# A retention-plus-experts kernel: batch 0 loaded ahead of the held weights, batch 1's attention moved later in tile 0, fp32 loads with casts on the engines

## Chip, cores, metric

One core of a Trainium2 chip; the rounds ran on several chips, each with the kernel before beside it for the ratio. The metric is the device time of the kernel in microseconds (us). Most executions of one kernel agree to about 0.3%.

Engine names: PE is TensorE, PEld its weight loads, DVE is VectorE, ACT is ScalarE, POOL is GpSimd, SP is SyncE (here only an issuer of DMAs). "Eviction" is the copy of a PSUM tile to SBUF through ACT.

## The reference

Retention attention over 8 batches of 8 heads, 576 positions, 64 dims; its output, as 4608 tokens of 512 features, goes through 4 experts (512 to 1024 to 512, ReLU) that are mixed with given probabilities.

```python
def _attn_ref(q, k, v):                      # (8, 8, 576, 64) each
    scores = scale * np.matmul(q, k.transpose(0, 1, 3, 2))
    Dmat = np.where(rel >= 0, gamma[:, None, None] ** rel[None, :, :], 0.0)
    return np.matmul(scores * Dmat[None], v)

def _moe_ref(x, domain_probs, w1, w2):       # (4608, 512), (4608, 4), (4, 512, 1024), (4, 1024, 512)
    p = domain_probs / (domain_probs.sum(-1, keepdims=True) + 1e-09)
    for e in range(E):
        out += p[:, e:e + 1] * (np.maximum(x @ w1[e], 0.0) @ w2[e])
```

## The kernel before

Nine token tiles of 512 go through the experts. While tile nt runs, the attention of batch nt+1 is woven in, one "unit" (a transpose group, a score group, a state step, an output group) after every second step of the tile. A tile has 48 steps: for each expert eight evictions of the first product (`ph` to `hT`) and four second products (`po`). Weights are cast to bf16 by the DMA.

```python
    load_first()                 # batch 0: k, v, q, two heads at a time, fp32, 24 DMAs on SP's queue
    ...
    for e in range(E):
        load_w(e)                # two cast DMAs of 512 K elements each, on POOL's queue, at once
        if e == 0:
            load_first_rem()
    ...
    nc.sync.dma_start(out=probs, ...)          # behind batch 0 on SP's queue
    # ... cut ...
    def load(b):                 # b >= 1
        for h in range(H):
            nc.sync.dma_start(out=t["k"][:, :, h, :], in_=main_in(k, b, h))       # fp32
        for n, src in (("q", q), ("v", v)):
            for h in range(H):
                nc.gpsimd.dma_start(out=m[:, :, h, :], in_=main_in(src, b, h))    # cast in flight
    # ... cut ...
    att = attention(0)
    next(att)
    next(att)                    # batch 0 up to its last output
    load(1)
    for nt in range(n_nt):
        if nt == 0:
            for _ in att:        # rest of batch 0
                pass
        nxt = attention(nt + 1) if nt + 1 < B else None
        if nxt is not None and nt + 2 < B:
            load(nt + 2)
        n = 0
        for _ in moe(nt):
            n += 1
            if nxt is not None and n >= 3 and n % 2 == 1:
                next(nxt, None)  # batch 1's first units come in expert 0 of tile 0
```

Of the kernel before, what the change touches and what calls it, by code (L numbers as in the profile page):

```python
# [2 lines left out]

# [6 lines left out]
FP32 = mybir.dt.float32  # L10
BF16 = mybir.dt.bfloat16
Copy = mybir.ActivationFunctionType.Copy
Relu = mybir.ActivationFunctionType.Relu
Exp = mybir.ActivationFunctionType.Exp
MULT = mybir.AluOpType.mult
ADD = mybir.AluOpType.add
# [4 lines left out]
def kernel(  # L21
# [10 lines left out]
    nc = tc.nc  # L32
    B, H, S, D = q.shape
    N, E = moe_domain_probs.shape
    _, Dm, F = moe_w1.shape
# [3 lines left out]
    NC_ = S // C  # L39
    R = S - NC_ * C  # L40
    SM = NC_ * C
    NP = H // 2
# [6 lines left out]

    const = ctx.enter_context(tc.tile_pool(name="const", bufs=1))  # L50
    wpool = ctx.enter_context(tc.tile_pool(name="wpool", bufs=1))
    raw = ctx.enter_context(tc.tile_pool(name="raw", bufs=3))
    rawr = ctx.enter_context(tc.tile_pool(name="rawr", bufs=2))
    cast2 = ctx.enter_context(tc.tile_pool(name="cast2", bufs=2))
    att1 = ctx.enter_context(tc.tile_pool(name="att1", bufs=1))
    att2 = ctx.enter_context(tc.tile_pool(name="att2", bufs=2))
    hpool = ctx.enter_context(tc.tile_pool(name="hpool", bufs=2))
    apool = ctx.enter_context(tc.tile_pool(name="apool", bufs=5))
    ps_mm = ctx.enter_context(tc.tile_pool(name="ps_mm", bufs=3, space=PSUM))
    ps_at = ctx.enter_context(tc.tile_pool(name="ps_at", bufs=4, space=PSUM))  # L60
    ps_kv = ctx.enter_context(tc.tile_pool(name="ps_kv", bufs=1, space=PSUM))
# [2 lines left out]
    def main_in(src, b, h):  # L64
        return src[b, h, 0:SM, :].rearrange("(c p) d -> p c d", p=C)

    def rem_in(src, b):
        return src[b, :, SM:S, :].rearrange("h p d -> p h d")

    state = {}  # L70

    def load_first():
        t = {}
        for n, src in (("k", k), ("v", v), ("q", q)):
            t[n] = raw.tile([128, NC_, H, D], FP32, tag="raw", name=f"raw_{n}")
        for p in range(NP):
            for n, src in (("k", k), ("v", v), ("q", q)):
                for h in (2 * p, 2 * p + 1):
                    nc.sync.dma_start(out=t[n][:, :, h, :], in_=main_in(src, 0, h))  # L79
        t["kr"] = rawr.tile([R, H, D], FP32, tag="rawr", name="rawr_k")  # L80
        nc.sync.dma_start(out=t["kr"], in_=rem_in(k, 0))
        state[0] = t

    def load_first_rem():
        for n, src in (("q", q), ("v", v)):
            r = cast2.tile([R, H, D], BF16, tag=f"{n}r", name=f"{n}r")
            nc.gpsimd.dma_start(out=r, in_=rem_in(src, 0))
            state[0][n + "rm"] = r

    def load(b):  # L90
        t = {}
        t["k"] = raw.tile([128, NC_, H, D], FP32, tag="raw", name="raw_k")
        t["kr"] = rawr.tile([R, H, D], FP32, tag="rawr", name="rawr_k")
        for h in range(H):
            nc.sync.dma_start(out=t["k"][:, :, h, :], in_=main_in(k, b, h))
        nc.sync.dma_start(out=t["kr"], in_=rem_in(k, b))
        for n, src in (("q", q), ("v", v)):
            m = cast2.tile([128, NC_, H, D], BF16, tag=f"{n}m", name=f"{n}m")
            r = cast2.tile([R, H, D], BF16, tag=f"{n}r", name=f"{n}r")
            for h in range(H):  # L100
                nc.gpsimd.dma_start(out=m[:, :, h, :], in_=main_in(src, b, h))  # L101
            nc.gpsimd.dma_start(out=r, in_=rem_in(src, b))
            t[n + "m"], t[n + "rm"] = m, r
        state[b] = t

    load_first()


    w1_sb, w2_sb = [], []

    def load_w(e):
        wt1 = wpool.tile([128, NDC, F], BF16, tag=f"w1_{e}", name="wt1")
        nc.gpsimd.dma_start(out=wt1, in_=moe_w1[e].rearrange("(dc p) f -> p dc f", p=128))
        w1_sb.append(wt1)
        wt2 = wpool.tile([128, NFC, Dm], BF16, tag=f"w2_{e}", name="wt2")
        nc.gpsimd.dma_start(out=wt2, in_=moe_w2[e].rearrange("(fc p) d -> p fc d", p=128))
        w2_sb.append(wt2)


    ident = const.tile([128, 128], BF16)  # L120
# [9 lines left out]
    gk = const.tile([128, NC_ + 1, H], FP32)  # L130
# [18 lines left out]
    for n in range(NC_):  # L149
        nc.vector.memset(sbd[n], 0.0)  # L150

    for e in range(E):
        load_w(e)
        if e == 0:
            load_first_rem()


    NTT = N // 128
    probs = const.tile([128, NTT, E], FP32)
    nc.sync.dma_start(out=probs, in_=moe_domain_probs.rearrange("(t p) e -> p t e", p=128))  # L160
    psm = const.tile([128, NTT], FP32)
    nc.vector.tensor_reduce(psm, probs, axis=mybir.AxisListType.X, op=ADD)
    nc.vector.tensor_scalar_add(psm, psm, 1e-9)
    nc.vector.reciprocal(psm, psm)
    nc.vector.tensor_tensor(probs, probs, psm[:, :].unsqueeze(2).to_broadcast([128, NTT, E]), op=MULT)

    xT = const.tile([128, NDC, N], BF16)

# [1 line left out]
    def attention(b):  # L170
        t = state[b]
        first = b == 0
        km = att1.tile([128, NC_, H, D], BF16, tag="km")
        kr = att1.tile([R, H, D], BF16, tag="kr")
        if first:
            qm = cast2.tile([128, NC_, H, D], BF16, tag="qm", name="qm")
            qr, vr = t["qrm"], t["vrm"]
            vm = cast2.tile([128, NC_, H, D], BF16, tag="vm", name="vm")
        else:
            qm, qr, vm, vr = t["qm"], t["qrm"], t["vm"], t["vrm"]  # L180

        def cast_k(h0, h1):
            n = h1 - h0
            for c in range(NC_):
                nc.vector.tensor_tensor(  # L185
                    km[:, c, h0:h1, :], t["k"][:, c, h0:h1, :],
                    gk[:, c, h0:h1].unsqueeze(2).to_broadcast([128, n, D]), op=MULT)

        def cast_first(p):
            h0, h1 = 2 * p, 2 * p + 2  # L190
            cast_k(h0, h1)
            nc.scalar.activation(qm[:, :, h0:h1, :], t["q"][:, :, h0:h1, :], Copy)  # L192
            nc.gpsimd.tensor_copy(vm[:, :, h0:h1, :], t["v"][:, :, h0:h1, :])

        def cast_rem():
            nc.vector.tensor_tensor(
                kr, t["kr"], gk[:R, NC_, :].unsqueeze(2).to_broadcast([R, H, D]), op=MULT)

        qkT = att1.tile([128, 2, NP, S], BF16, tag="qkT")
        kvp = {}  # L200
# [87 lines left out]
        allp = list(range(NP))  # L288
        if first:
            def start(p):  # L290
                cast_first(p)
                U_T(p)
                U_kv(0, [p])

            def mid(p):
                U_S(p)
                for n in range(1, NC_):
                    U_kv(n, [p])
            start(0)
            mid(0)  # L300
            start(1)
            U_O(0)
            mid(1)
            start(2)
            U_O(1)
            yield
            mid(2)
            start(3)
            U_O(2)
            mid(3)  # L310
            U_O(3)
            yield
            cast_rem()
            U_Trem()
            yield
            U_Srem()
            yield
            U_Orem()
            yield
        else:  # L320
            cast_k(0, H)
            cast_rem()
            yield
            for u in (lambda: U_T(0), lambda: U_kv(0, allp), lambda: U_T(1), lambda: U_kv(1, allp),
                      lambda: U_S(0), lambda: U_kv(2, allp), lambda: U_T(2), lambda: U_S(1),
                      lambda: U_O(0), lambda: U_T(3), lambda: U_kv(3, allp), lambda: U_S(2),
                      lambda: U_O(1), U_Trem, lambda: U_S(3), lambda: U_O(2), U_Srem,
                      lambda: U_O(3), U_Orem):
                u()
                yield  # L330


    def moe(nt):
        n0 = nt * NT
        acc = [apool.tile([128, Dm], FP32, tag="acc", name="acc") for _ in range(NSUB)]
        for e in range(E):
            hT = hpool.tile([128, NFC, NT], BF16, tag="hT")
            for fc in range(NFC):
                ph = ps_mm.tile([128, NT], FP32, tag="mm", name="ph")
                for dc in range(NDC):  # L340
                    nc.tensor.matmul(ph, lhsT=w1_sb[e][:, dc, fc * 128:(fc + 1) * 128],  # L341
                                     rhs=xT[:, dc, n0:n0 + NT], start=(dc == 0), stop=(dc == NDC - 1))
                nc.scalar.activation(hT[:, fc, :], ph, Relu)  # L343
                yield
            for ns in range(NSUB):
                po = ps_mm.tile([128, Dm], FP32, tag="mm", name="po")
# [11 lines left out]

    att = attention(0)
    next(att)  # L360
    next(att)
    load(1)
    for nt in range(n_nt):
        units = []
        if nt == 0:
            for _ in att:
                pass
        nxt = attention(nt + 1) if nt + 1 < B else None
        if nxt is not None and nt + 2 < B:
            load(nt + 2)  # L370
        n = 0
        for _ in moe(nt):
            n += 1
            if nxt is not None and n >= 3 and n % 2 == 1:
                next(nxt, None)
        if nxt is not None:
            for _ in nxt:
                pass


# [28 lines left out]
```

## Time and profile before

| | before |
|---|---|
| median time | 641.65 us (16 runs, 639.82 to 642.91) |
| span of the profiled run | 640.1 us |
| PE busy | 572.1 us |
| PE without work | 68.0 us |
| first eviction of tile 0 | 82.38 us |
| period of a tile with attention (first eviction of tile 2 to that of tile 3) | 63.41 us |

PE is the busy engine, so its idle time is the account that most of a gain must come from. The view of busy time by stretch divides it (columns: stretch, length, then busy time of PE, PEld, DVE, ACT, POOL with instruction counts, granted clock, DMA share, GB/s):

```profile
0.00:64.00 64.00, 3.70 (x32) 2.37 (x32) 8.45 (x42) 7.29 (x12) 13.76 (x27) 1.00 1.11 185
64.00:82.38 18.38, 14.58 (x123) 7.79 (x122) 12.27 (x23) 6.55 (x30) 15.25 (x21) 0.98 1.78 168
82.38:145.24 62.86, 62.86 (x408) 29.86 (x408) 24.78 (x39) 24.31 (x44) 23.14 (x32) 0.98 0.97 110
145.24:640.10 494.86, 490.96 (x2961) 231.18 (x2958) 159.21 (x242) 190.25 (x336) 53.21 (x72) 1.00 0.23 33
```

Length minus PE busy is PE's idle time: 60.3 us before 64 us, 3.8 us up to the first eviction, nothing in tile 0, and 3.9 us after it (the tail of the last tile). So nearly all of the 68.0 us lies before the experts begin.

### The profile page before, as it was taken

Reading aid. Unit: us, or ns where it says so; the run is one execution under the profiler, and the core shown is the slowest. Engines: PE = TensorE matmul, PEld = TensorE weight load, DVE = VectorE, ACT = ScalarE, POOL = GpSimd, SP = SyncE. Lnnn points to the kernel's source line nnn. Section 1 sums busy time; section 2 is a strip of 40 time slices with the busy share of each in tenths; the row PEclk is TensorE's granted clock in tenths of the full one; section 3 lists DMA queues with packets and bytes.
Section 4 is the critical chain, followed back from the end, with each engine's and each line's share of the span. In section 5 each row is a group of like instructions: output and inputs, shape, how many; then the busy total and the mean of one; then the engine's idle time right before and its main releaser. Section 6 shows DMA issues by size and latency. Waiting matters only on the chain.

```text
span 640.1 us, 8432 instructions
## 1 busy us (share of the span) xinstructions
PE 572.1 (89%) x3520; PEld 271.2 (42%) x3520; DVE 204.7 (32%) x345; ACT 228.4 (36%) x422; POOL 105.4 (16%) x150
## 2 busy tenths in 40 slices
PE   0110889999999999999999999999999999999997
PEld 0000444444444444444444444454444444444443
DVE  1200633631463146314631463146313420121121
ACT  0300444325332533253325333533353235333332
POOL 5101860440034003401240124000000000000000
PEclk9999989999999999999999999999999999999999
DMA  9999996960096009600570047000100010001001
GB/s 165 193 201 179 166 178 98 111 67 37 1 112 70 34 1 112 72 32 5 42 86 18 6 32 87 18 1 1 52 14 1 1 66 1 2 1 67 0 1 66
DMA packets 130165, 38.36 MB, mean 60 GB/s; under 512 B 119376, under 2 KB 123472, under 8 KB 130128
## 3 DMA queue, kind: packets, MB, share of 16 engines
q0 software_dynamic: 73856, 16.79, 28.2%
q1 hardware_dynamic: 56272, 21.05, 14.8%
q8 instruction: 27, 0.44, 0.3%
q14 instruction: 10, 0.08, 0.0%
HBM read 45.16 MB, written 9.44 MB: 85 GB/s over the span
## 4 chain that ended last, share of the span: by engine, by line
PE 87%; SPq 9%; DMA 2%; POOL 2%; issue 0%; DVE 0%; POOLq 0%
PE ph L341 39%; PE po L348 39%; SPq L79 9%; PE pt L220 2%; PE o L267 2%; PE s L242 1%; DMA vm<-in_v_dram 1%; PE o L271 1%; PE kvp L207 1%; POOL qm L101 1%; DMA raw_v<-in_v_dram 1%; POOL vm L101 1%; PE ptr L229 0%; PE orem L280 0%; PE orem L284 0%; PE sr L255 0%
## 5 line engine op out<-in xcount | busy, mean ns | idle before, releaser
L343 ACT ACTIVATE hT<-ph 128x512 bf16<-128x512 f32 x288 | 171.9, 597 | 299.5 <-PE ph L341 298.2
L341 PE MATMUL ph<-xT,wt 128*128 128x512 bf16 x1152 | 272.9, 381 | 1.4 <-DVE xT L274 1.4
L348 PE MATMUL po<-wt,hT 128*128 128x512 bf16 x1152 | 261.4, 379 | 0.0
L348 PEld LDWEIGHTS <-hT 128*128 128x128 bf16 x1152 | 110.7, 98 | 126.7
L341 PEld LDWEIGHTS <-wt 128*128 128x128 bf16 x1152 | 107.4, 98 | 118.1 <-issue 2.1
L354 DVE SCALAR_TENSOR_TENSOR acc<-po,probs,acc 128x512 f32<-128x512 f32 x108 | 81.1, 751 | 197.8 <-PE po L348 179.6
L101 POOL DMA_DIRECT2D qm<-in_q_dram x56 | 41.7, 771 | 158.1 <-PE pt L220 155.1
L246 DVE TENSOR_TENSOR sT<-s,tri 128x512 bf16<-128x512 f32 x64 | 41.1, 683 | 53.5 <-PE s L242 53.5
L101 POOL DMA_DIRECT2D vm<-in_v_dram x56 | 41.7, 772 | 60.9 <-PE o L271 58.2
L223 DVE COPY qkT<-pt 128x1024 bf16<-128x1024 bf16 x32 | 22.0, 688 | 88.4 <-PE pt L220 88.4
L220 PE MATMUL pt<-ident,qm 128*128 128x128 bf16 x128 | 13.6, 232 | 32.3 <-ACT qm L192 32.3
L207 PE MATMUL kvp<-vm,km 128*128 128x128 bf16 x128 | 15.5, 226 | 27.9 <-ACT sbd L213 25.8
L352 ACT ACTIVATE acc<-po,probs 128x512 f32<-128x512 f32 x36 | 24.7, 687 | 36.8 <-PE po L348 36.8
L185 DVE TENSOR_TENSOR km<-raw_k,gk 128x512 bf16<-128x512 f32 (+1 forms) x44 | 21.4, 542 | 40.5 <-DMA raw_k<-in_k_dram 23.0
L213 ACT ACTIVATE sbd<-kvp 64x256 bf16<-64x256 f32 (+1 forms) x88 | 27.8, 316 | 8.7 <-PE kvp L207 8.1
L274 DVE TENSOR_TENSOR xT<-o,gq 128x512 bf16<-128x512 f32 x32 | 22.0, 686 | 21.5 <-PE o L271 19.5
L220 PEld LDWEIGHTS <-qm 128*128 128x128 bf16 x128 | 10.3, 103 | 39.5 <-ACT qm L192 32.6
L267 PEld LDWEIGHTS <-vm 128*64 128x64 bf16 x256 | 8.8, 111 | 40.0 <-issue 39.9
L192 ACT ACTIVATE qm<-raw_q 128x512 bf16<-128x512 f32 x4 | 2.5, 629 | 39.4 <-DMA raw_q<-in_q_dram 39.4
L242 PE MATMUL s<-qkT 64*128 64x128 bf16 x256 | 13.8, 226 | 2.4 <-DVE qkT L223 2.4
L267 PE MATMUL o<-sT,vm 128*64 128x128 bf16 x256 | 15.0, 231 | 0.0
L207 PEld LDWEIGHTS <-km 128*128 128x128 bf16 x128 | 10.5, 100 | 10.4 <-issue 2.2
(48 smaller groups left out, 117.5 us busy)
## 6 DMA issues: line engine op xcount, KB each, us to landing
out_dram<-acc SPq DMA_DIRECT2D x36, 256.0 KB, 2.0
raw_k<-in_k_dram SPq DMA_DIRECT2D x64, 128.0 KB, 4.6
wt<-in_moe_w_dram POOLq DMA_DIRECT2D x8, 1024.0 KB, 31.1
qm<-in_q_dram POOLq DMA_DIRECT2D x56, 64.0 KB, 3.1
vm<-in_v_dram POOLq DMA_DIRECT2D x56, 64.0 KB, 3.0
raw_v<-in_v_dram SPq DMA_DIRECT2D x8, 128.0 KB, 10.5
raw_q<-in_q_dram SPq DMA_DIRECT2D x8, 128.0 KB, 14.5
rawr_k<-in_k_dram SPq DMA_DIRECT2D x8, 128.0 KB, 3.6
```

The costliest lines, as they stand in the source:

```text
L79: nc.sync.dma_start(out=t[n][:, :, h, :], in_=main_in(src, 0, h))
L101: nc.gpsimd.dma_start(out=m[:, :, h, :], in_=main_in(src, b, h))
L207: nc.tensor.matmul(kvp[g][:, p, :], lhsT=km[:, n, 2 * p:2 * p + 2, :].rearrange("p h d -> p (h d)"), rhs=vm[:, n, 2 * p:2 * p + 2, :].rear ...
L213: nc.scalar.activation(sbd[n][j:j + 64, a:z, j:j + 64], kvp[g][j:j + 64, a:z, j:j + 64], Copy)
L220: nc.tensor.transpose(pt[:, i, c * C:(c + 1) * C], src[:, c, 2 * p:2 * p + 2, :].rearrange("p h d -> p (h d)"), ident)
L246: nc.vector.tensor_tensor(st[:, j], s[j], tri[:, :].unsqueeze(1).to_broadcast([128, NC_, C]), op=MULT)
L267: nc.tensor.matmul(o[64 * j:64 * j + 64, c * C:(c + 1) * C], lhsT=vm[:, c, 2 * p + j, :], rhs=sT[p][:, j, c, :], start=(c == 0), stop=Fals ...
L341: nc.tensor.matmul(ph, lhsT=w1_sb[e][:, dc, fc * 128:(fc + 1) * 128], rhs=xT[:, dc, n0:n0 + NT], start=(dc == 0), stop=(dc == NDC - 1))
L343: nc.scalar.activation(hT[:, fc, :], ph, Relu)
L348: nc.tensor.matmul(po, lhsT=hT[:, fc, ns * 128:(ns + 1) * 128], rhs=w2_sb[e][:, fc, :], start=(fc == 0), stop=(fc == NFC - 1))
L352: nc.scalar.activation(acc[ns], po, Copy, scale=pe)
L354: nc.vector.scalar_tensor_tensor(acc[ns], po, pe, acc[ns], op0=MULT, op1=ADD)
```

## The change

Its intent: give the DMA engines to batch 0 alone at the start, let the weights follow when they are about to be needed, keep all of q, k, v off POOL's queue, and move batch 1's attention to where its data will have arrived. The diff, cut to its core:

```diff
+    nc.sync.dma_start(out=probs, ...)          # the probabilities go first
+    load(0)
...
-    def load_first(): ...   def load_first_rem(): ...   # q, v of b >= 1 by cast DMAs on POOL's queue
+    def load(b):                               # every batch: 24 fp32 DMAs on SP's queue, one buffer each
+    def after(ins, dep): ...                   # an extra semaphore wait of ins on dep
...
+        def cast_pair(p):                      # one cast of a pair on DVE (k), ACT (q) and POOL (v)
+            ck = nc.vector.tensor_tensor(km..., MULT)
+            cq = nc.scalar.activation(qm[:, :, h0:h1, :], t["q"][:, :, h0:h1, :], Copy)
+            gate[b, p] = nc.gpsimd.tensor_copy(vm[:, :, h0:h1, :], t["v"][:, :, h0:h1, :])
+            if b == 1:
+                for i in (ck, cq, gate[b, p]):
+                    after(i, evict[2 + p // 2, 7 if p < 2 else 3])
...
     att = attention(0)
     next(att)
+    w = [load_w(0)]
+    for i in w[0]:
+        after(i, gate[0, 2])                   # weights only after the v cast of batch 0's pair 2
     next(att)
+    w += [load_w(e) for e in range(1, E)]      # (held in the same way)
+    mixing_weights()
+    load_rem(0)
+    for i in load(1)[:1]:
+        after(i, w[0][1])                      # batch 1 after expert 0's second matrix has landed
+    load_rem(1)
     for nt in range(n_nt):
...
+            if nt == 0:
+                if n in (11, 13, 15, 17):
+                    next(att, None)            # the rest of batch 0, inside expert 0 and 1
+                if n == 33 or n == 42:
+                    next(nxt)                  # casts of batch 1, in expert 2 and 3
+                elif n == 44:
+                    next(nxt); load(2); load_rem(2)
+                elif n > 44:
+                    next(nxt, None); next(nxt, None)   # two units per step; the other 11 after the tile
+            else:
+                if n == 12 and nt + 2 < B:
+                    load(nt + 2); load_rem(nt + 2)
+                if n >= 3 and n % 2 == 1:
+                    next(nxt, None)
```

The accumulator pool also goes from 5 to 7 buffers, and the k cast of a pair is one instruction instead of four.

## The prediction

> **What bounds the kernel now.** I read the page from its forty slices, then asked for the first microseconds (what SyncE's queue issues, who waits), then for the period of the steady part.
>
> The slices come first, because the average PE share (89%) hides two different stages:
>
> ```profile
> span 640.1 us, 8432 instructions
> PE 572.1 (89%) x3520; PEld 271.2 (42%) x3520; DVE 204.7 (32%) x345; ACT 228.4 (36%) x422; POOL 105.4 (16%) x150
> PE   0110889999999999999999999999999999999997
> ACT  0300444325332533253325333533353235333332
> DMA  9999996960096009600570047000100010001001
> ```
>
> One slice is 16 us. In the first four (0 to 64 us) PE does almost nothing while the DMA engines are full; from about 86 us on PE has no gap until the end. So there is a start bounded by DMA and then a long stretch bounded by TensorE. The busy time by stretch shows how tight the second is:
>
> ```profile
> 145.24:208.65 63.41, 63.41 (x410) 30.20 (x408) 23.91 (x37) 24.42 (x44) 13.30 (x18) 1.00 0.44 55
> 462.29:525.70 63.41, 63.41 (x409) 30.20 (x408) 20.91 (x32) 24.43 (x44) 0.00 (x0) 1.00 0.05 17
> 525.70:580.96 55.26, 55.26 (x257) 25.05 (x256) 9.01 (x12) 21.86 (x36) 0.00 (x0) 1.00 0.05 20
> ```
>
> The columns are the stretch, its length, then busy time of PE, weight loads, DVE, ACT, POOL, granted clock, DMA share and GB/s. One token tile that also carries a batch of attention takes 63.41 us, all of it PE; a tile without attention takes 55.26; the difference, 8.15 us, is PE work of one batch. Tile 1 starts at 145.24. From there to the end are six tiles of 63.41, two of 55.26 and 3.9 us of tail: 494.9 us, and 145.24 + 494.9 = 640.1. These 494.9 us only change if a tile's period does. The whole question is when tile 1 starts.
>
> The stretch before that is held up by loads. The waits:
>
> ```profile
> ACT qm L192 <- DMA raw_q<-in_q_dram: 39.4, 3, 23.5
> POOL vm L193 <- DMA raw_v<-in_v_dram: 38.9, 3, 24.5
> PE pt L220 <- ACT qm L192: 32.3, 2, 19.1
> PE kvp L207 <- ACT sbd L213: 25.8, 2, 25.6
> ```
>
> The casts of batch 0 wait for its q and v, and PE waits for the casts. The last q of batch 0 landed at 62.8 us though it is only 3.1 MB. The queues between 14 and 57 us say why:
>
> ```profile
> DMA packets 12504, 8.48 MB, mean 197 GB/s; under 512 B 7399, under 2 KB 10968, under 8 KB 12504
> q0 software_dynamic: 6257, 6.93, 93.0%
> q1 hardware_dynamic: 6247, 1.55, 27.7%
> ```
>
> q0 brings the weights (cast in flight, so 6.93 MB landed are 13.86 MB read), q1 the first batch in rows of 256 B. Both moved the same number of packets, and so q1 got 1.55 of 8.48 MB: the first batch, needed at once, was spread over the whole weight load, most of which is needed much later.
>
> **What the Trainium skill says.** "DMA: Bandwidth & Descriptors", section "Queues, rings and completion order": each DMA engine goes round-robin between its queue rows packet by packet. The trace agrees: 6257 against 6247 packets. The same page, "Specifications", puts a core's HBM limit at about 358 GB/s; here 13.86 + 1.55 MB read in 43 us are 358 GB/s, so this stage is at that limit. The same page, "SWDGE vs HWDGE vs iDMA": a cast during DMA can only be issued from GpSimd. The trace agrees: q and v of batches 1 to 7, which are cast, run as POOL's issues at about 0.74 us each. "TensorE: Matmul & The Clock Gate", "What's actually happening": after an idle window the array runs at half clock until it has been busy a few us. The trace shows the first 512-column matmuls after the idle start at 0.44 to 0.58 us a piece, against 0.216 later (6.91 us for 32), so the restart costs one or two us.
>
> **The change part by part.**
> (1) *Order of the loads.* Probabilities first, then batch 0 alone, then the weights (held until the cast of v of pair 2), then batch 1 (held until expert 0's second matrix has landed). The probabilities are 4608 packets of 16 B; before, they kept the queue at some 30 GB/s for about 3.5 us near 63 us. So batch 0 flows from about 6 us. In a quiet queue SyncE issues a 128 KB load every 0.53 to 0.57 us (seven in 3.97 us): 24 loads are 13 us, all landed by about 20 us instead of 62.8. v of pair 2 lands near 15.5, so weights start near 17; expert 0's two matrices, nearly alone, take about 5.9 us each by 2.1 MB / 358 GB/s: landed near 25 and 30. The other six share with batch 1: by the before's 161 GB/s landed, 1.05 MB each, 6.5 us each: 36.5, 43, 49.5, 56, 62.5, 69. Batch 1 gets 145 packets/us meanwhile, 5700 of 13,824 by 69 us, and the remaining 8100 at about 1000 a us: landed near 79.
> (2) *Attention of batch 0.* q of pair 0 lands near 10.5; then table load 1.28, cast 0.63, the two exponentials 3.35: ACT is free for the state copies at 15.8. Each copy-accumulate step took 0.8 to 0.9 us in the trace (64.15, 65.06, 65.86, 66.69); four pairs of four steps plus casts bring the last xT to about 36. In the new instruction order six matmuls of the first expert stand before pair 3's transposes; they want the first weights at about 26, which are there at about 25. The rest of expert 0's first product ends near 40.5.
> (3) *Tile 0.* Expert 0 done at 40.5 + 6.9 + 0.9 (rest of batch 0) = 48.3; experts 1 and 2, 13.8 each: 75.9; first product of expert 3: 82.8. Weights are always 7 to 10 us ahead. The casts of batch 1 now stand in ACT's and DVE's own order before the sixth eviction of expert 3; they need batch 1 at 78 to 80, so about no stall. Second product of expert 3 with six units of attention 1: 6.9 + 2.6, to 92.3.
> (4) *What is lost again.* The other attention units of batch 1 are no longer spread over tile 0; they follow it in a lump. They hold 9.6 us of DVE work (T 0.69, sT 1.3, xT 0.69 each, as in the groups), with about 4.5 us of PE work inside, so PE waits some 5 us: last xT near 102, less about 2 us of tile-1 matmuls already slipped in: tile 1 starts in effect near 100.
> (5) *Steady state.* q and v of every batch come as fp32 on SyncE's queue and are cast:
>
> ```profile
> L192 ACT ACTIVATE qm<-raw_q 128x512 bf16<-128x512 f32 x4 | 2.5, 629 | 39.4 <-DMA raw_q<-in_q_dram 39.4
> L193 POOL CAST vm<-raw_v 128x512 bf16<-128x512 f32 x4 | 2.5, 618 | 38.9 <-DMA raw_v<-in_v_dram 38.9
> L343 ACT ACTIVATE hT<-ph 128x512 bf16<-128x512 f32 x288 | 171.9, 597 | 299.5 <-PE ph L341 298.2
> ```
>
> Per tile ACT gains 4 x 0.63 + about 0.4 = 2.9 us on 24.4 of 63.4; POOL loses 17 issues. The new order puts the four q casts into expert 2's eight evictions: 8 x 0.60 + 4 x 0.63 + 0.77 = 8.1 us of ACT in a stretch in which PE needs 6.9 + 4 x 0.4 = 8.5. With three PSUM buffers that costs 0 to 0.3 us a tile; I take 1.5 us over six tiles.
> Sum: 100 + 494.9 + 1.5 = 596.4 of span; the time stands 1.9 above the span (642.0 against 640.1): 598.3.
>
> **The rivals.**
> (a) *The loads are hidden anyway*: tile 0 was slow for PE, not DMA, and the gain is small. Against it: PE busy digits 0, 1, 1, 0. It would leave about 640; I give it almost nothing.
> (b) *Batch 1 lands late and becomes the new wait.* It is fp32 now, 3.5 MB against 256-byte packets that lose the round-robin. ACT executes in order, so a late q holds up evictions of expert 3 and with them PE. Every us after 81 costs a us; if it lands at 90, the time is 607. For it: packets at parity in the trace. Against it: 10 us of weights' lead that the sharing can spend.
> (c) *ACT or DVE binds in steady state*: if the casts wait for something in a place where evictions stand behind them, each of six tiles could lose 1 to 2 us, so 604 to 609. Against it: ACT is only 39% busy.
> (d) *The start is shorter*: the chain in (2) runs faster and the lump in (4) is better filled: tile 1 at 92, time 590.
>
> **Range and chances.** The start can hardly cost more than 12 us above my sum, as the volume of 23.9 MB at 358 GB/s alone is 67 us and all else follows it; nor can tile 1 start before about 30 + 63 = 93. With (b), (c) and (d): 598, between 589 and 609. Faster by over 2% (below 629) 0.97, within 2% 0.02, slower 0.01.
>
> **What would show each step right or wrong.** Last q of batch 0 landing at 19 to 22 us, first weights at about 25, batch 1 whole at 77 to 83. First eviction of tile 0 at 33 to 37, instead of 82.4. PE about solid from 36 to 92, then a ragged patch of some 9 us, then solid. Tile period 63.4 to 63.8. Tile 1 at about 100. PE busy time about unchanged. I would be wrong if ACT's longest waits name batch 1's or batch 2's q with PE idle beside it, if weights land after PE wants them, or if a tile's period is over 64.5.

## The result

| | before | changed |
|---|---|---|
| median time | 641.65 us (16 runs) | 596.59 us (8 runs, 595.77 to 598.2) |
| span of the profiled run | 640.1 us | 594.2 us |
| PE busy | 572.1 us | 571.6 us |
| PE idle | 68.0 us | 22.6 us |
| first eviction of tile 0 | 82.38 us | 34.43 us |
| period of a tile with attention | 63.41 us | 63.41 us |

The ratio is 0.9303 (95% interval 0.929 to 0.9317). A ratio is the mean time of one kernel's fast runs over that of the other's of the same rounds, so not quite the ratio of the medians quoted. The page of the changed kernel begins so (two of its rows of slices are shown):

```profile
span 594.2 us, 8579 instructions
PE 571.6 (96%) x3520; PEld 271.7 (46%) x3520; DVE 204.2 (34%) x333; ACT 246.4 (41%) x458; POOL 34.9 (6%) x58
PE   1799999999999999999999999999999999999997
DMA  9999988936410344007500850000000010000001
```

A slice is 14.9 us now. PE's row has one low digit at the start instead of four, while DMA's first slices are as full as before: the same loads, in another order. ACT is 18.0 us busier (228.4 before) and POOL 70.5 us less busy, since the casts and their issues moved; neither is near its span. The same view by stretch as above, for the changed kernel:

```profile
0.00:20.00 20.00, 5.77 (x50) 3.60 (x51) 9.13 (x34) 8.21 (x20) 6.14 (x17) 1.00 1.03 168
20.00:34.43 14.43, 10.96 (x86) 5.83 (x87) 7.73 (x12) 5.53 (x23) 4.91 (x7) 1.00 1.16 195
34.43:91.30 56.87, 56.62 (x313) 26.25 (x312) 16.53 (x25) 27.13 (x48) 6.04 (x6) 1.00 1.09 200
91.30:102.20 10.90, 10.23 (x138) 6.34 (x136) 10.06 (x19) 3.95 (x8) 2.76 (x5) 1.00 0.91 234
102.20:594.20 492.00, 488.04 (x2940) 229.64 (x2939) 160.77 (x246) 201.56 (x361) 15.02 (x26) 1.00 0.22 54
```

PE's idle time is 14.2 us before 20 us, 3.5 up to the first eviction, 0.25 in tile 0, 0.67 in the stretch after it in which batch 1's last units stand in a lump, and 4.0 after that. Against before, the 64.1 us of idle ahead of the first eviction have become 17.7, and nearly nothing came back later. That difference, 46.4, less the 1.0 that did come back, is the 45.4 us by which PE's idle time shrank; PE's busy time is the same to 0.5 us.

Idle time is not the whole account, because matmuls that follow each other slowly count as busy. Priced at the mean spacing that each kind of matmul has in the changed kernel from 227 to 480 us, the matmuls that start between 91.36 and 102.2 us are 8.3 us of work, and they take 10.8. From the start of the first `po` matmul to the first eviction of tile 2 the same pricing gives 120.4 us of work in 120.4 us for the kernel before, and 122.0 in 124.3 for the changed one. So the lump costs some 2.3 us, of which PE's idle time shows 0.67.

The waits that answer to those of before (columns: total us, times, longest us):

```profile
PE pt L207 <- ACT qm L171: 13.0, 3, 11.7
ACT L171 <- DMA raw_q<-in_q_dram: 9.8, 1, 9.8
ACT qm L171 <- DMA raw_q<-in_q_dram: 5.5, 3, 3.1
POOL vm L172 <- DMA raw_v<-in_v_dram: 14.3, 5, 6.2
```

The prediction shows the waits of before but for one, that of ACT's table load:

```profile
ACT L192 <- DMA raw_q<-in_q_dram: 17.1, 1, 17.1
```

What was 56.5 us (39.4 and 17.1) of waits for q and 38.9 for v is 15.3 and 14.3. Of these, 3.06 and 1.43 belong to batch 1, and 2.5 of the waits for q to batch 2. The queues between 20 and 70 us (packets, MB, share):

```profile
q0 software_dynamic: 6205, 8.25, 92.9%
q1 hardware_dynamic: 6800, 1.69, 24.4%
```

The same unequal sharing as before (6205 packets carry 8.25 MB, 6800 carry 1.69 MB), but the queue that loses is now bringing batch 1, which has until about 80 us, and no longer batch 0. When it arrives can be seen on ACT's timeline (start, length; the bracket is ACT's idle time before it and what ended it):

```profile
34.43 2.31 ACT L333 ACTIVATE hT<-ph 128x512 bf16<-128x512 f32 x4 [1.84 <-PE ph L331]
...
72.79 0.63 ACT L171 ACTIVATE qm<-raw_q 128x512 bf16<-128x512 f32 x1 [3.06 <-DMA raw_q<-in_q_dram]
...
82.10 0.63 ACT L180 ACTIVATE qr<-raw_qr 64x512 bf16<-64x512 f32 x1 [0.52 <-DMA raw_qr<-in_q_dram]
```

Of batch 1's four q casts only the second waited for a DMA, 3.06 us up to 72.79, in a stretch in which no eviction was due (the next, at 76.24, itself waited 2.82 us for PE). Its last piece, the remainder of q at 82.10, had 0.52 us to wait, with evictions behind it. The steady state, by stretch (most of tile 2 and the start of tile 3):

```profile
164.70:228.10 63.40, 63.40 (x409) 30.19 (x408) 23.81 (x37) 26.77 (x50) 2.90 (x5) 1.00 0.29 71
```

PE is busy for the whole of it, as before: the added 2.35 us of ACT (24.42 in the tile that the prediction shows, 26.77 now) cost PE nothing.

### The profile page after: what moved, and what is told of

It reads as the page before. It is cut to its first block, busy times and chain, and to the rows that moved or that the text cites. A ratio compares the mean times of both kernels' runs of the same rounds, so it can differ in the third digit from the quotient of the medians.

```text
span 594.2 us, 8579 instructions
## 1 busy us (share of the span) xinstructions
PE 571.6 (96%) x3520; PEld 271.7 (46%) x3520; DVE 204.2 (34%) x333; ACT 246.4 (41%) x458; POOL 34.9 (6%) x58
## 4 chain that ended last, share of the span: by engine, by line
PE 95%; ACT 2%; DVE 1%; SPq 1%; DMA 1%; issue 0%; DVEq 0%; ACTq 0%
PE ph L331 42%; PE po L340 42%; PE pt L207 2%; PE o L254 2%; PE s L229 2%; PE kvp L194 2%; PE o L258 1%; SPq L79 1%; DMA raw_q<-in_q_dram 1%; ACT sbd L200 0%; ACT gq L139 0%; PE ptr L216 0%; PE sr L242 0%; PE orem L267 0%; DVE xT L261 0%
## 5 line engine op out<-in xcount | busy, mean ns | idle before, releaser
L331 PE MATMUL ph<-xT,wt 128*128 128x512 bf16 x1152 | 270.0, 381 | 1.2 <-DVE xT L261 0.9
L172 POOL CAST vm<-raw_v 128x512 bf16<-128x512 f32 x32 | 20.2, 663 | 356.0 <-PE o L254 290.0
L168 DVE TENSOR_TENSOR km<-raw_k,gk 128x512 bf16<-128x512 f32 x32 | 21.9, 734 | 21.6 <-ACT hT L333 10.0
L171 ACT ACTIVATE qm<-raw_q 128x512 bf16<-128x512 f32 x32 | 19.5, 625 | 8.5 <-DMA raw_q<-in_q_dram 5.5
L180 ACT ACTIVATE qr<-raw_qr 64x512 bf16<-64x512 f32 x8 | 5.0, 628 | 27.6 <-PE ptr L216 27.1
L254 PE MATMUL o<-sT,vm 128*64 128x128 bf16 x256 | 14.2, 230 | 0.5 <-DVE xT L261 0.4
L229 PEld LDWEIGHTS <-qkT 64*128 64x128 bf16 x256 | 7.8, 97 | 14.0 <-issue 11.5
```

Of the source, the lines that this page charges most:

```text
L229: nc.tensor.matmul(s[j][:, c, :], lhsT=qkT[r, 1, p, cs], rhs=qkT[r, 0, p, cs], start=True, stop=True)
L254: nc.tensor.matmul(o[64 * j:64 * j + 64, c * C:(c + 1) * C], lhsT=vm[:, c, 2 * p + j, :], rhs=sT[p][:, j, c, :], start=(c == 0), stop=Fals ...
L331: nc.tensor.matmul(ph, lhsT=w1_sb[e][:, dc, fc * 128:(fc + 1) * 128], rhs=xT[:, dc, n0:n0 + NT], start=(dc == 0), stop=(dc == NDC - 1))
```

## The experiments

The theory after the result had two halves. (1) The *hold* of the weights lets batch 0 land early; (2) the *later place* of batch 1's attention keeps PE from waiting for a batch that cannot be there yet. Rivals: that the hold alone gives the gain; that the fp32 loads, which keep q and v off POOL's queue, do; that the hold of batch 1 does. A last group asks what binds the 17.7 us of start that are left. Time and ratio are against the kernel before in the same rounds.

### The hold alone, on the kernel before

```diff
-    for e in range(E):                      # weights no longer at once, but
-        load_w(e)
+    for i in load_w(0): after(i, gate[2])   # each after the v cast of batch 0's pair 2
...
+    for i in load(1): after(i, w0[1])       # batch 1 after expert 0's second matrix
```

> The kernel before with one part of the change alone: the weights wait for the cast of v of pair 2 of batch 0, and batch 1's loads wait for expert 0's second matrix. Loads of q and v still cast in flight on the weights' queue, and the attention of batch 1 keeps its old place in tile 0. Theory (order of the loads gives the start, but the placing of batch 1's attention must follow it): batch 0 complete by about 18 us and the first eviction of tile 0 near 33 us, but PE then stops at batch 1's attention, whose q and v queue behind the weights and land at 70 to 80 us; total 605 to 620 us. Rival A (the order alone is the whole gain): 594 to 600. Rival B (the gain comes from loading q and v as fp32 and casting on the engines): 635 to 642.

Measured: 626.74 us, ratio 0.9789 (0.9774 to 0.9803). The waits of this kernel show why it missed:

```profile
DVE psm L167 <- DMA probs<-in_moe_domain_probs_dram: 31.1, 1, 31.1
PE o L272 <- DVE sT L251: 31.0, 1, 31.0
```

The probabilities were still issued on SP's queue behind batch 1's loads, which now wait, so they arrived late; DVE works in order, so everything of batch 0 behind the mixing weights stood still, and PE with it for 31 us. An edit of mine, not the place of batch 1's attention, set this time. It is a confounded run, and it shows why the change moves the probabilities to the front.

### The hold with the probabilities first

The same, plus

```diff
+    nc.sync.dma_start(out=probs, ...)       # ahead of batch 0
```

> The kernel before with the hold as in a_hold_only, and with the probabilities loaded first, as in the change. In a_hold_only the probabilities stood behind batch 1's held loads on SyncE's queue, and DVE, which has their sums ahead of batch 0's work, stopped for 31 us; so that run did not test the place of batch 1's attention. Now it should: batch 0 and expert 0 run from about 30 us, then PE stops near 47 us at batch 1's first transposes until its q has landed (63 to 70 us, behind all weights) and again for v (70 to 76). Theory: 604 to 620 us. Rival A (order of the loads is the whole gain): 594 to 600.

Measured: 625.19 us, ratio 0.9762 (0.9743 to 0.9781), 5 us above the range. The expected mechanism is there: batch 0 and expert 0's first product run early, then PE waits for batch 1, whose first units the old order has in expert 0 of tile 0. The wait, POOL's issues, and the stretch in which PE stands:

```profile
PE pt L225 <- DMA qm<-in_q_dram: 22.5, 2, 21.5
POOL qm L101 <- DMA wt<-in_moe_w_dram: 39.4, 7, 8.1
```

```profile
52.20:73.77 21.57, 0.07 (x2) 0.04 (x2) 2.30 (x4) 0.60 (x1) 3.70 (x5) 0.61 1.27 191
```

PE works 0.07 us of 21.57. What I had underrated is when the weights are through. The last of them landed at 71.14 us, and batch 1's first two q loads, issued at 34.92 and 35.66 on the same queue, landed behind it at 72.39 and 73.63 (63 to 70 had been expected). PE went on at 73.77. POOL's later issues each waited for a weight to land (seven waits, up to 8.1 us), but the two loads that PE waited for had long been issued. With batch 1's attention in its old place the new order of loads is worth about 15 us of the 45.

### The changed kernel without the hold

```diff
+    w = [load_w(e) for e in range(E)]       # all weights at once, at the start
     att = attention(0)
-    w = [load_w(0)] ... after(i, gate[0, 2]) ...
```

> The changed kernel with the hold on the weights taken away: all eight weight transfers are issued at the start, everything else as changed. Theory (the hold is the main term): the last q of batch 0 lands at 62 to 67 us again, the first eviction of tile 0 is at 66 to 74, tile 1 starts near 140, total 630 to 643 us. Rival B (fp32 loads and the later place of batch 1's attention make the gain): 594 to 606.

Measured: 640.99 us, ratio 1.0009 (0.9994 to 1.0024): the whole gain is gone. PE's slices, then two entries of ACT's timeline:

```profile
PE   0011899999999999999999999999999999999997
```

```profile
64.21 0.63 ACT L171 ACTIVATE qm<-raw_q 128x512 bf16<-128x512 f32 x1 [3.15 <-DMA raw_q<-in_q_dram]
79.67 2.31 ACT L333 ACTIVATE hT<-ph 128x512 bf16<-128x512 f32 x4 [1.74 <-PE ph L331]
```

The last q of batch 0 is cast at 64.21 and the first eviction comes at 79.67, near the 82.38 of before (66 to 74 had been expected). Later placement, fp32 loads and probabilities first gain nothing while batch 0 shares the engines with the weights.

### Batch 1's attention early again

```diff
-            if b == 1:
-                ... after(i, evict[2 + p // 2, 7 if p < 2 else 3])
...
-                if n == 33 or n == 42: ...
+                if n in (19, 21, 23) or n >= 30:
+                    next(nxt, None)
```

> The changed kernel with the place of batch 1 undone: its casts and attention units may come from unit 19 and 30 of tile 0 on, without the waits that kept them behind expert 2's and 3's evictions; loads and holds as changed. The casts now stand in ACT's order between evictions of expert 0 and 1, ahead of data that lands at 57 to 82 us. Theory (in-order engines turn a late load into a stop of PE): PE stands from about 45 to 70 us or longer, total 612 to 632 us. Rival (the place does not matter once the loads are in the new order): 592 to 600.

Measured: 621.81 us, ratio 0.971 (0.9695 to 0.9724). The hold is untouched here. ACT's timeline, and PE's wait:

```profile
62.40 0.63 ACT L171 ACTIVATE qm<-raw_q 128x512 bf16<-128x512 f32 x1 [23.92 <-DMA raw_q<-in_q_dram]
```

```profile
PE po L337 <- ACT hT L330: 22.7, 1, 22.7
```

ACT stands for 23.92 us at batch 1's first q, the evictions stand behind it, and PE waits 22.7 us for the eviction. This is rival (b) of the prediction, and it is real: the place of the casts is what avoids it. With the two runs above, the halves do not add: hold without place gains 15 to 19 us, place without hold nothing, both 45.

### q and v cast in flight again

The loads of q and v of batches 1 to 7, and all remainders of q and v, go back to cast DMAs on POOL's queue (from batch 1 on, behind the weights), the accumulator pool back to 5 buffers; order and places stay.

```diff
+    def load_cast(b):                       # b >= 1: k fp32 on SP's queue,
+        ... nc.gpsimd.dma_start(out=m[:, :, h, :], in_=main_in(src, b, h))   # q, v cast in flight
```

> The changed kernel with the fp32 loads undone: q and v of batches 1 to 7 and their remainders are cast in flight on GpSimd's queue again, held behind expert 0's second matrix and so behind all weights; hold, places and k as changed; five output buffers as before. Theory (fp32 loading and casting on the engines is nearly neutral; it only changes what batch 1 queues behind): batch 1 lands at 78 to 86 us, tile period 63.4, total 593 to 604 us. Rival B (fp32 loading is a main term): over 612.

Measured: 597.41 us, ratio 0.9333 (0.9317 to 0.9349), where the changed kernel has 0.9303. Most of tile 2 and the start of tile 3:

```profile
162.84:226.25 63.41, 63.41 (x410) 30.24 (x408) 23.82 (x37) 24.41 (x44) 13.29 (x18) 1.00 0.44 55
```

The period is 63.41 with POOL at 13.29 us of issues, as it was with the casts on the engines. The fp32 loads are not where the bulk of the gain is from. The two ratios differ by 0.003, or 1.9 us, and their intervals just touch, so that 0 to some 4 us may hang on them.

### The changed kernel again, and with batch 1 not held

A repeat, for the spread between chips:

> The changed kernel once more, on the same chip as the three that follow, so that they have something to be measured against: 0.930 of the kernel before, tile 1 in effect at 99 to 100 us.

Measured: 596.22 us, ratio 0.9299 (0.9279 to 0.932). Then without the wait on batch 1:

```diff
-    for i in load(1)[:1]:
-        after(i, w[0][1])
+    load(1)
```

> The changed kernel with batch 1's loads not held behind expert 0's second matrix; the order of instructions on every engine stays as it is. The loads then share the DMA engines with expert 0's matrices from 19 us on. The volume is the same, so batch 1 lands at most 2 us earlier; expert 0's first matrix lands 0.5 to 2 us later, at 27 to 28 us, and PE wants it at 26.4. Theory: 0 to 2 us slower than the changed kernel (0.930 to 0.934 of before). Rival (the hold is needed): over 600 us.

Measured: 596.42 us, ratio 0.931 (0.9293 to 0.9327): no difference. That batch 1 waits for expert 0's second matrix is worth nothing that these runs can tell.

### What binds the start that is left: the exponentials

In the changed kernel ACT's table load waits for q of pair 0 until 9.76 us, and the exponentials of the decay factors come after it. Here they come first:

```diff
+            if b == 0 and p == 0:
+                after(cq, last_exp)         # first q cast after the exponentials
```

> The changed kernel, with ACT's exponentials (table load 1.28, 0.22 and 3.13 us, which stood behind the first cast of q, and so behind its landing at 9.8 us) put ahead of that cast. Nothing else is edited. The step tested: the chain of batch 0's attention on ACT sets when tile 0 starts. If that chain alone sets the end: 3 to 4 us less. My theory is that two further things bind within 1 us of it: expert 0's first matrix lands at 26.3 us, and batch 1's last remainder at 82 us, which the sixth eviction of expert 3 waits for. Then the first eviction of tile 0 comes 1 to 3 us earlier, expert 3's evictions stop for that long at 79 to 82 us, and the total is 0 to 1 us less than the changed kernel.

Measured: 597.01 us, ratio 0.9319 (0.9296 to 0.9343): nothing. First eviction 34.46 against 34.43. PE's largest wait between 20 and 40 us, and a piece of the chain that ended last (start, length):

```profile
PE ph L333 <- DMA wt<-in_moe_w_dram: 2.2, 1, 2.2
```

```profile
16.72 9.22 DMA wt<-in_moe_w_dram
```

With ACT's chain shortened, PE comes earlier to its first expert matmuls, which the order has in front of pair 3's transposes, and waits there for the first matrix. Two chains had ended within 2 us of each other.

### What binds the end of the start: the last matrix held back

Expert 3's second matrix waits for batch 1's loads, so that batch 1 is whole earlier and its units can be spread over expert 3; casts of batch 2 stay out of the way.

```diff
-        for i in w[e]:
+        for i in w[e][:2 if e < E - 1 else 1]:
...
+    after(w[E - 1][1], l1[-1])
...
-                if n == 33 or n == 42:       # casts of batch 1 at 33, 34, 36, a unit per step from 37
```

> The changed kernel, with expert 3's second matrix held until batch 1's last main load has landed, batch 1's casts put behind expert 2's first product, its attention units spread over expert 3 (one for each eviction) instead of in a lump at its end, and batch 2's casts put into tile 1. Tests the lump: by the trace of the changed kernel PE needs 61.8 us from 35.1 us on for what it has to do before tile 1, which gives 96.9, and tile 1 in effect starts at 99.3, so the lump costs 2.4 us. Theory: batch 1 whole at 75 to 78 us, ragged patch gone, 1 to 2.5 us less than the changed kernel. Rival: the second matrix now lands too late (83 us or more) and PE waits for it: 0 to 3 us more.

Measured: 596.3 us, ratio 0.9318 (0.9288 to 0.9347). Batch 1 was whole at 76.7 us as expected, and the lump after tile 0 was down from 11 units to 3; 1 to 2.5 us less had been expected, but the time is the same. Both edits together:

> f and g together. If f's gain is swallowed by batch 1's late landing, it must come out here, where batch 1 lands earlier: 3 to 5 us less than the changed kernel, about 591.5 to 593.5 us. If f and g are independent, the two gains just add. If expert 0's first matrix binds the start, f's part is at most 1 us.

Measured: 595.86 us, ratio 0.9295 (0.9275 to 0.9315); 3 to 5 us less had been expected. Its chain shows a small new wait, for v's casts on POOL; on POOL's timeline the issue of the held matrix waits 33.56 us for batch 1's q, until 75.18, and the casts stand behind it in that engine's order:

```profile
76.92 1.73 POOL vm L174 x3
```

### All of attention 0 before the first expert matmul

To separate "the first matrix binds" from "attention 0 binds", the exponentials go first as above and expert 0's first matmuls may start only after batch 0's last score copy:

```diff
+                    if nt == 0 and e == 0 and dc == 0 and fc < 3:
+                        after(mm, gate["s", 0, NP - 1])
```

> The exponentials come before the first q cast, and expert 0's first product may start only after the last S transpose copy of batch 0, so that all of TensorE's work for attention 0 is done before it. If the start alone binds (attention behind expert 0's first matrix), the first eviction comes at about 27 to 28 us instead of 34.4 and the kernel is 5 to 6 us faster than the changed one. If the landing of batch 1 (82 us, set by the volume of loads) binds as well, expert 3's last evictions wait for its last q cast, and only 0 to 2 us remain: the first eviction still comes at 27 to 28, expert 3's first product is done by about 76 and its last two evictions are at about 82.

Measured: 596.6 us, ratio 0.9316 (0.9298 to 0.9333). And with the last matrix held too:

> As the run before it, and expert 3's second matrix is held until batch 1's main loads have landed, so batch 1 is whole at about 77 us and the second matrix at about 83; the units of attention 1 are spread, eight of them ahead of expert 3's second product. If start and batch 1's landing are the two binders, tile 1 is in effect at 94 to 97 us instead of 99.3 and the total 591 to 594 (3 to 5 us under the changed kernel). If a third thing binds (the second matrix itself, or VectorE's work for attention 1), the total stays within 1.5 us of the changed kernel.

Measured: 596.49 us, ratio 0.9313 (0.9297 to 0.9329). The expectation for the start missed: the first eviction of the first of the two came at 33.47 us, not at 27 to 28. Of the second, the branch in which a third thing binds came true. The chains of the changed kernel and of this one:

```profile
26.43 2.64 PE ph L331 x6
...
39.55 5.18 PE po L340 x24
```

```profile
30.28 0.58 PE o L256 x7
...
31.51 8.34 PE ph L333 x31
```

With no expert matmul in its way, and no wait for the matrix, attention 0 still takes until 31.3 us; then the first product runs in one piece. It takes 8.34 us for 32 matmuls, for which 6.91 would do at the steady rate, because its first seven come 0.43 us apart instead of 0.216. The view by stretch shows it, in PE's count:

```profile
31.50:34.50 3.00, 2.99 (x7) 1.05 (x7) 0.59 (x1) 0.60 (x1) 0.00 (x0) 1.00 1.17 206
34.50:39.00 4.50, 4.50 (x22) 2.05 (x21) 0.00 (x0) 2.98 (x5) 0.00 (x0) 1.00 1.14 204
```

The product ends at about 39.8, against 39.55 in the changed kernel, where nine of those matmuls fill gaps of attention 0. So my two binders were both wrong as *the* binder: a third chain, attention 0's own, ends at the same time. In this run it begins with the loads (k of pair 2 landed at 14.5 us) and goes on as a hand-over from PE to DVE, ACT and back. Something I did not test belongs to it: PE runs at half its later pace in it. In the changed kernel its 128-column transposes come 107 ns apart up to 29.5 us, and 56 ns apart later. The granted clock reads 1.00 there too, so that column does not show it, and how much of the start hangs on it is open.

Span minus the start of the first `po` matmul gives one number for the rest of each run:

| run | us |
|---|---|
| changed kernel; without the hold; exponentials early; both edits | 554.8 to 554.9 |
| repeat, batch 1 not held | 554.7 |
| this run; the same with the matrix held | 555.0; 554.9 |
| casts in flight | 554.6 |
| last matrix held alone | 554.0 |
| batch 1 early | 580.3 |
| kernel before | 550.9 |

So what comes after the first product is the same in all runs with the new places, except where PE has to wait for batch 1. A shorter start would show in an earlier first `po` matmul; it comes between 39.4 and 40.6 us in all runs with the hold and the new places. What comes after is not PE's work alone: the lump's 2.3 us are in it. (The kernel before has 1.6 us of attention work ahead of that matmul which the changed kernel has behind it; the rest of the difference is the lump.) Holding the last matrix took 0.8 us from it at best, which timing with this spread does not resolve. Some traces of this group lack up to 2% of the matmul records, so their busy sums are not compared.

## Why the prediction was right

The time (598 against 596.59) and the mechanism were right; by its own steps:

1. *Order of the loads.* The last q of batch 0 landed at 20.3 us, and the last v cast came at 19.4 (said: all landed by about 20). Weights were issued at 16.69 (17), the first matrix landed at 26.3 (25). The second landed at 33.5 instead of 30: the two matrices do not come "nearly alone", as the last batch-0 pieces and the other experts' loads share with them; the third matrix is issued at 20.00. Batch 1 was whole at 82.0 instead of 79, inside the 77 to 83 given; the prediction's own terms (8100 packets at 1000 a us after 69) make 77. Between 20 and 70 us 8.25 MB landed by cast, 16.5 MB read, and 1.69 MB make 364 GB/s, 2% above the figure that the prediction took for the limit. That the hold is necessary is shown by the run without it.
2. *Attention of batch 0.* Last output at 33.3 to 34.0 instead of 36; first eviction 34.43 (33 to 37); first product done at 39.55 (40.5). The terms given (15.8, 16 steps of 0.85, four casts) make 32; how they become 36 is not said. In the trace the six expert matmuls stand in between for 2.5 us. The restart of PE was foreseen for the expert matmuls, by comparing durations of 0.44 to 0.58 us with a spacing of 0.216; spacing with spacing it is 0.43, six times in the changed kernel (1.3 us more), and it holds for attention 0's matmuls too, which was not seen. Nor was it that three chains (ACT's, the first matrix's, attention 0's own) end together, so that shortening one of them alone gained nothing.
3. *Tile 0.* Expert 3's first product ended at 82.25 (82.8), the second product with its units at 91.33 (92.3). Batch 1's casts waited 3.06 and 0.52 us on ACT, and PE's idle time in the whole stretch from 34.43 to 91.30 was 0.25 us: no stall, as said. That this place is necessary is shown by the run with batch 1 early, 25 us slower.
4. *What is lost again.* I booked some 5 us of PE waiting in the lump, less about 2 of early tile-1 work: 3 net. PE's idle time there was only 0.67 us, but its matmuls came slowly, and the loss is some 2.3 us, so the net term was near. DVE was the full engine, as said (10.06 of 10.90 us), and PE had the attention work and tile 1's matmuls on each finished pair in between. Tile 1 began in effect at 99.3 (162.71, the start of tile 2, less 63.41), against 100: 8.0 us after tile 0's second product instead of 7.7.
5. *Steady state.* I booked 1.5 us over six tiles for the q casts among the evictions; the period is 63.41, as before, so 0. This term was mis-sized.

The sum: tile 1 0.7 us earlier, 1.5 us not lost, and a time 1.8 above the span instead of 1.9 (596.04 for the profiled run) make 2.3 us less than the 598.3 of the working. The terms missed in both directions, by up to 3.5 us (the second matrix); that the total is nearer than its terms is luck.

Of the rivals, (a) is refuted by the result. (b) is real but avoided with nothing to spare (batch 1 whole at 82.0, expert 3's first product done at 82.25); with batch 1 early it costs 25 us. (c), ACT or DVE binding in steady state, did not happen. (d) did not happen, and the last group of runs shows why it would be hard: from 20 us on PE is idle for only 4.4 us up to 102.2. (Its 92 for tile 1 also lies below the 93 that the prediction's range gives as the earliest.)

What stays open: what the half pace of PE costs in the start, whether fp32 loading is worth anything (0 to 4 us), and what the accumulator buffers and the k cast in one instruction do, which no run changes alone.

## What to carry to other kernels

Account a start by the idle time of the engine that is busy afterwards, and ask which of the bytes in the queues is needed first; here the order of the loads, with the place of batch 1's attention, was worth 45 us with no work removed. Such a hold pays only if the consumers are moved to where the delayed data will be: in an engine that works in order, one early cast of a late batch stops everything behind it. When a fix to one chain of a start gives nothing, look whether two others end at the same time before planning the next fix.

## What the Trainium skill lacked or had wrong

- "DMA: Bandwidth & Descriptors", "Queues, rings and completion order", gives the round-robin between queue rows by packet, but not what follows for unequal packets: in the changed kernel between 20 and 70 us 6800 packets of the fp32 queue carried 1.69 MB while 6205 of the cast queue carried 8.25 MB. Here the queue of 256-byte rows, each of which the profile counts as a packet, got about a sixth of the bytes landed.
- No page I read says that issues of cast DMAs from GpSimd can stand behind earlier ones until these land: in the hold with the probabilities first, with eight weight loads issued, seven later issues each waited for a weight to land, up to 8.1 us (39.4 us in all). The cause of the limit is not shown by these runs.
- "TensorE: Matmul & The Clock Gate", "Back-to-back issue gap", gives about 131 ns per 512-column matmul as the sustained spacing. Here 32 of them take 6.91 us in the steady part, 216 ns each, with their weight loads hidden; that is the page's formula for an isolated gap, and what the same page measured back to back elsewhere, not the sustained figure of this section.
- "DMA: Bandwidth & Descriptors" treats small rows but has no figure for rows of 16 bytes: with the 4608 packets of the probabilities ahead of them, SP's first two loads of batch 0 took 3.55 us to issue, against 1.06 for the next two, and 0.98 in the kernel before, where nothing stood ahead of them.
